# Cached decode attention, two blocks: wq streamed per group, selector matmuls replaced by a DVE transpose, QK matmuls widened

## Chip, cores and metric

The kernel runs on one core of a Trainium2 chip. The metric is the device time of one execution in microseconds (us); runs of one kernel agree within 0.3%, most within 0.1%. Times quoted are medians. "Profile" means the trace of one execution, and the times read from it are from that execution's own start.

The engines in it are PE (TensorE, matrix multiplication; PEld is its loading of the stationary operand), DVE (VectorE), ACT (ScalarE), POOL (GpSimd) and SP (SyncE, which here issues the loads). The loads themselves are moved by 16 DMA engines. QK is the multiplication of the query with the keys, PV that of the probabilities with the values. PSUM is the memory into which PE writes. A slot is on-chip memory for one tile.

## The reference

Two independent blocks, A and B, do the same with their own inputs; the outputs are concatenated.

```python
B, Sq, D = 8, 1, 1024;  H, Sk, Dh = 32, 4096, 128      # all bfloat16
q      = (x @ wq) as [B, H, 1, Dh]
scores = einsum("bhqd,bhkd->bhqk", q, k_cache) * Dh ** -0.5
p      = softmax(scores)
o      = einsum("bhqk,bhkd->bhqd", p, v_cache)
out    = o as [B, 1, H * Dh] @ wo
```

One query per batch means that every key and value is used once: 2 blocks x 32 heads x 8 batches x 2 caches = 1,024 tiles of 1 MB, and besides them 16 MB of wq and 16 MB of wo. The profile counts 1,107 MB read.

## The kernel before

All loads are issued by SP in one fixed order: x and all of wq, then for every head 8 key tiles, a slice of wo, 8 value tiles. A load waits only until its slot is free.

```python
NK = 5                                                   # key slots
NV = 6                                                   # value slots
# ...
wq_sb = sb("wq_sb", [128, NCH, HD], BF16)                # all 8 MB of one block
q_pad = sb("q_pad", [128, NBLK, HD], BF16)
l32 = sb("l32", [128, 2, 8, 4, 32], BF16)
# ... SP:
def prologue_loads(blk):
    # blk 0: wait for the constants, blk 1: for the q of block A
    sp.dma_start(x_sb[0:Bsz, blk, :], x[:, 0, :]).then_inc(s_x[blk], 16)
    for ch in range(NCH):
        sp.dma_start(wq_sb[:, ch, :], wq[ch * 128:(ch + 1) * 128, :]).then_inc(s_wq[blk], 16)
prologue_loads(0)
for n in range(NH):
    for b in range(Bsz):
        wait(sp, s_tr, t - NK + 1)                       # slot free: its tile is transposed
        sp.dma_start(knat[:, slot, :], kc[b, h]...)
    # ... wo
    for b in range(Bsz):
        wait(sp, s_pv, t - NV + 1)                       # slot free: its PV is done
        sp.dma_start(vnat[:, slot, :], vc[b, h]...)
    if blk == 0 and h == H_PRO:                          # head 15: x and wq of block B
        prologue_loads(1)
```

Per key tile, DVE transposes it (2.31 us by the page) and PE multiplies. The stationary operand `l32` has 32 columns, and four matmuls at a time go to four column groups of the array, where they run side by side: the 4,096 columns of a tile took 0.66 us at full clock, and 1.91 us in the changed kernel, whose QK has no column groups:

```python
for c in range(4):
    for g in range(4):
        pe.matmul(S_ps[par][32 * g:32 * g + 32, :], lhsT=l32[:, par, b, c, :],
                  rhs=ktv[:, 8 * g:8 * g + 8, bq, :, e_],          # 256 columns
                  start=(b == 0 and c == 0), stop=(b == Bsz - 1 and c == 3),
                  tile_position=(0, 32 * g))
```

After the eight tiles of a head there is a chain: row maximum (DVE), exchange of the maximum over partitions (PE, DVE, PE), exp (ACT), then the probabilities are brought to the layout that PV needs by 32 selector matmuls and an ACT copy:

```python
for jj in range(8):
    for a_ in range(4):
        pe.matmul(Pn_ps[32 * a_:32 * a_ + 32, jj * 32:(jj + 1) * 32],
                  lhsT=e_sb[:, jj * 32:(jj + 1) * 32], rhs=sel[:, a_, :], ...)
# ACT: pn_sb <- Pn_ps
```

PV is 8 matmuls of 512 columns per value tile, with 4-column stationary operands, batch b in column group b % 4. The output projection adds one head's part to PSUM.

## Time and profile before

| | before |
|---|---|
| time, median of 3 runs | 2685.14 us |
| DMA, steady state | about 419 GB/s, engines 90% busy or more in all slices but the first and the last |
| PE, DVE, ACT busy | 57%, 47%, 10% |
| mean granted PE clock | 0.695 |

From the page of the kernel before: busy time of each engine, then the 40 slices of the span (PEclk is the granted PE clock and DMA the busy share of the 16 DMA engines, in tenths), then two DMA queues with packets, MB and share of 16 engines' span.

```profile
PE 1542.8 (57%) x17024; PEld 603.9 (22%) x17024; DVE 1269.5 (47%) x717; ACT 273.3 (10%) x791; POOL 12.3 (0%) x17
...
PEclk9767767667676776766766767767767667667667
DMA  6999999999999999999999999999999999999998
GB/s 284 409 420 420 418 419 419 418 419 416 420 420 419 419 415 420 417 419 420 416 419 418 419 417 419 416 420 420 419 420 417 420 420 416 418 418 420 413 421 355
...
q1 hardware_dynamic: 159008, 1107.40, 99.7%
q8 instruction: 135, 2.21, 0.3%
```

The DMA row is full except in the first and last slice, and the load queue q1 fills 99.7% of the engines' time. So the kernel waits for bytes, and only two things can shorten it: engines that carry loads in more of the span, or loads that cost the engines less. q8 is the fetch of instructions, 135 packets of 16 KB.

Where the loads are missing is seen in the windows of the start (busy time of PE, weight loads, DVE, ACT, POOL with counts, then granted clock, DMA share, GB/s) ...

```profile
core 0: us, PE busy (x) PEld busy (x) DVE busy (x) ACT busy (x) POOL busy (x), PEclk, DMA share, GB/s
0.00:10.00 10.00, 0.00 (x0) 0.00 (x0) 3.88 (x8) 0.00 (x0) 9.41 (x7) 1.00 0.00 0
10.00:20.00 10.00, 0.38 (x32) 0.33 (x32) 0.90 (x5) 1.51 (x2) 2.90 (x11) 1.00 0.55 209
...
50.00:60.00 10.00, 4.58 (x84) 2.46 (x86) 4.80 (x3) 2.27 (x6) 0.00 (x0) 0.92 0.38 133
```

... and in the timeline of the kernel before (start, duration, engine, line, operation, count):

```profile
2.53 6.93 POOL L193 MEMSET q_pad<- 128x8192 bf16 x1
...
13.01 0.40 SPq L160 DMA_DIRECT2D x_sb<-in_A_x_dram  x1
13.47 4.02 SPq L162 DMA_DIRECT2D wq_sb<-in_A_wq_dram  x8
...
17.53 3.92 SPq L172 DMA_DIRECT2D knat<-in_A_k_cache_dram  x4
```

The first load is issued at 13.0 us, behind POOL's fill of q_pad. At 50 to 60 us the share falls to 0.38: the key slots are full, and PE is still making q for all 32 heads.

Two readings of PE from the middle of the run: a value tile's 8 matmuls, and a key tile's 16 at full and at half clock.

```profile
1003.75 1.89 PE L361 MATMUL ps<-vnat,pn_sb 128*4 128x512 bf16 x8 [0.59 <-DMA vnat<-in_A_v_cache_dram]
...
1011.07 0.66 PE L314 MATMUL ps<-kt,l 128*32 128x256 bf16 x16 [0.90 <-DVE kt L234]
...
1018.52 1.04 PE L314 MATMUL ps<-kt,l 128*32 128x256 bf16 x16 [1.43 <-DVE kt L234]
```

And the time from a load's issue to its landing (the last column, median), which says how much work the DMA engines have queued (a tile lands every 2.483 us, so 12.2 us are about five):

```profile
knat<-in_A_k_cache_dram SPq DMA_DIRECT2D x256, 1024.0 KB, 12.2
vnat<-in_A_v_cache_dram SPq DMA_DIRECT2D x256, 1024.0 KB, 15.3
```

A landing of a 1 MB tile every 2.483 us and 0.68 us for a head's slice of wo make 16 x 2.483 + 0.68 = 40.41 us per head. Every head has one reciprocal on DVE, so the first and the last of the 64 mark the start, the middle and the tail; these are the lines of the timeline before:

```profile
72.90 0.17 DVE L246 RECIPROCAL rlo_sb<-ps 128x2 f32<-128x2 f32 x1 [1.81 <-PE ps L343]
...
2663.07 0.17 DVE L246 RECIPROCAL rlo_sb<-ps 128x2 f32<-128x2 f32 x1 [1.81 <-PE ps L343]
```

The middle is 2663.07 - 72.90 = 2590.2 us. Take from it 63 heads of 40.41 us (2545.8) and the 8 MB of block B's wq (8 x 2.483 = 19.9), and 24.5 us are left. This is the **excess**.

### The profile page before, as it was taken

The page shows a single profiled execution, that of the slowest core. Times are in us where ns is not written, and L with a number is a line of the kernel's source. Part 1 is how long each engine was busy: PE and PEld are TensorE (multiplying, and loading weights), DVE is VectorE, ACT ScalarE, POOL GpSimd, SP SyncE. Part 2 cuts the span into 40 slices and gives each one's busy share as a digit, 9 for nine tenths or more (in the row PEclk, how much of TensorE's full clock was granted, in tenths as well). Part 3 has the DMA queues.
Part 4 walks back from the last instruction along what each step waited for, and adds up shares of the span by engine and source line. Part 5 has one row for each costly group of instructions (what it writes and reads, how often), then busy time and mean ns, then how long its engine had stood idle before and what let it go on. Part 6 is the DMA issues. An engine that isn't in the chain of part 4 may idle for free.

```text
span 2685.2 us, 38364 instructions
## 1 busy us (share of the span) xinstructions
PE 1542.8 (57%) x17024; PEld 603.9 (22%) x17024; DVE 1269.5 (47%) x717; ACT 273.3 (10%) x791; POOL 12.3 (0%) x17
## 2 busy tenths in 40 slices
PE   3655655656465565565665655655655656656555
PEld 1222222222122222222222222222222222222222
DVE  3455354354335435445445445355454454454453
ACT  1100100110011011000110100100100110001001
POOL 1000000000000000000000000000000000000000
PEclk9767767667676776766766767767767667667667
DMA  6999999999999999999999999999999999999998
GB/s 284 409 420 420 418 419 419 418 419 416 420 420 419 419 415 420 417 419 420 416 419 418 419 417 419 416 420 420 419 420 417 420 420 416 418 418 420 413 421 355
DMA packets 159237, 1109.89 MB, mean 413 GB/s; under 512 B 17712, under 2 KB 17744, under 8 KB 25952
## 3 DMA queue, kind: packets, MB, share of 16 engines
q1 hardware_dynamic: 159008, 1107.40, 99.7%
q8 instruction: 135, 2.21, 0.3%
q14 instruction: 30, 0.25, 0.0%
q10 hardware_dynamic: 64, 0.03, 0.0%
HBM read 1107.33 MB, written 0.03 MB: 412 GB/s over the span
## 4 chain that ended last, share of the span: by engine, by line
DMA 60%; PE 18%; DVE 14%; SPq 3%; issue 3%; ACT 1%; POOL 0%; POOLq 0%; DVEq 0%
DMA knat<-in_B_k_cache_dram 30%; DMA knat<-in_A_k_cache_dram 29%; DVE kt L234 11%; PE ps L361 11%; PE ps L314 3%; SPq L172 2%; DVE negm L242 2%; DVE m_sb L238 1%; PE ps L335 1%; SPq L183 1%; DMA wq_sb<-in_A_wq_dram 1%; PE ps L322 1%; PE ps L288 1%; PE ps L273 1%; PE ps L343 1%
## 5 line engine op out<-in xcount | busy, mean ns | idle before, releaser
L234 DVE STREAM_TRANSPOSE kt<-knat 128x2048 f32<-128x2048 f32 x512 | 1183.1, 2311 | 1173.1 <-DMA knat<-in_A_k_cache_dram 589.5
L361 PE MATMUL ps<-vnat,pn_sb 128*4 128x512 bf16 x4096 | 867.3, 436 | 120.7 <-DMA vnat<-in_A_v_cache_dram 60.1
L314 PE MATMUL ps<-kt,l 128*32 128x256 bf16 x8192 | 519.4, 397 | 699.7 <-DVE kt L234 697.8
L314 PEld LDWEIGHTS ps<-kt,l 128*32 128x32 bf16 x8192 | 225.3, 122 | 979.9 <-DVE kt L234 922.1
L361 PEld LDWEIGHTS ps<-vnat,pn_sb 128*4 128x4 bf16 x4096 | 289.0, 92 | 668.9 <-issue 172.9
L450 ACT ACTIVATE o_sb<-ps,rlo_sb 128x512 bf16<-128x512 f32 x128 | 81.0, 684 | 900.3 <-PE ps L361 900.3
L431 ACT ACTIVATE bias_sb<-ps 128x1 f32<-128x1 f32 x64 | 11.0, 171 | 1346.1 <-PE ps L327 1346.1
L419 ACT ACTIVATE l<-ps 32x32 bf16<-32x32 f32 x256 | 76.8, 300 | 33.8 <-PE ps L288 29.1
L372 PE MATMUL ps<-selrow,o_sb 128*128 128x4 bf16 x512 | 22.6, 166 | 87.0 <-ACT o_sb L450 87.0
L246 DVE RECIPROCAL rlo_sb<-ps 128x2 f32<-128x2 f32 x64 | 10.9, 171 | 115.9 <-PE ps L343 115.9
L238 DVE TENSOR_REDUCE m_sb<-ps 128x1 bf16<-128x256 f32 x64 | 27.3, 427 | 73.7 <-PE ps L314 73.7
L335 PE MATMUL ps<-sel,e_sb 128*32 128x32 bf16 x2048 | 26.0, 190 | 56.0 <-ACT e_sb L435 56.0
L242 DVE TENSOR_REDUCE negm<-ps 1x32 bf16<-1x512 f32 x64 | 43.4, 678 | 22.9 <-PE ps L322 22.9
L273 PE MATMUL ps<-wq_sb,xT_sb 128*8 128x512 bf16 x128 | 33.1, 416 | 36.2 <-DMA wq_sb<-in_A_wq_dram 20.7
L372 PEld LDWEIGHTS ps<-selrow,o_sb 128*128 128x128 bf16 x512 | 17.0, 96 | 119.2 <-ACT o_sb L450 119.2
L327 PE MATMUL ps<-scalecol,negm 128*32 128x1 bf16 x256 | 12.5, 186 | 49.3 <-DVE negm L242 49.3
L322 PE MATMUL ps<-ident,m_sb 128*1 128x128 bf16 x64 | 17.0, 266 | 34.2 <-DVE m_sb L238 34.2
L383 PE MATMUL ps<-wo_sb,oT_sb 128*8 128x512 bf16 x128 | 25.2, 390 | 17.1 <-ACT oT_sb L454 17.1
L335 PEld LDWEIGHTS ps<-sel,e_sb 128*32 128x32 bf16 x2048 | 19.1, 104 | 61.4 <-ACT e_sb L435 61.4
L288 PE MATMUL ps<-ident,q_pad 128*32 128x8 bf16 x1024 | 18.3, 172 | 24.2 <-DVE rlo_sb L246 24.2
L435 ACT ACTIVATE e_sb<-ps,bias_sb 128x256 bf16<-128x256 f32 x64 | 30.3, 474 | 2.1
L442 ACT ACTIVATE pn_sb<-ps 128x256 bf16<-128x256 f32 x64 | 24.6, 384 | 14.4 <-PE ps L335 14.4
(39 smaller groups left out, 151.1 us busy)
## 6 DMA issues: line engine op xcount, KB each, us to landing
knat<-in_A_k_cache_dram SPq DMA_DIRECT2D x256, 1024.0 KB, 12.2
vnat<-in_A_v_cache_dram SPq DMA_DIRECT2D x256, 1024.0 KB, 15.3
knat<-in_B_k_cache_dram SPq DMA_DIRECT2D x256, 1024.0 KB, 12.1
vnat<-in_B_v_cache_dram SPq DMA_DIRECT2D x256, 1024.0 KB, 15.5
wq_sb<-in_A_wq_dram SPq DMA_DIRECT2D x8, 1024.0 KB, 11.8
wo_sb<-in_A_wo_dram SPq DMA_DIRECT2D x32, 256.0 KB, 10.4
wq_sb<-in_B_wq_dram SPq DMA_DIRECT2D x8, 1024.0 KB, 16.9
wo_sb<-in_B_wo_dram SPq DMA_DIRECT2D x32, 256.0 KB, 10.4
```

The costliest lines, as they stand in the source:

```text
L172: sp.dma_start(knat[:, slot, :], kc[b, h].rearrange("(p j) d -> p (j d)", p=128),).then_inc(s_kld[slot], 16)
L234: dve.transpose(kt[:, ts, :].bitcast(F32), knat[:, ks, :].bitcast(F32)).then_inc(s_tr, 1)
L238: dve.tensor_reduce(m1_sb[:], S_ps[par], axis=AX.X, op=ALU.max).then_inc(s_m1, 1)
L242: dve.tensor_reduce(negm[0:1, :].rearrange("p (i a) -> p i a", i=8), r_in, axis=AX.XY, op=ALU.max, negate=True).then_inc(s_negm, 1)
L273: last = pe.matmul(q_ps[G % 2], lhsT=xT_sb[:, blk, ch, :], rhs=wq_sb[:, ch, gq * GW:(gq + 1) * GW], start=(ch == 0), stop=(ch == NCH - 1))
L288: last = pe.matmul(qW_ps[32 * a_:32 * a_ + 32, c * 8:c * 8 + 8], lhsT=q_pad[:, blk, base:base + 63:2], rhs=ident[:, 0:8], start=True, stop ...
L314: last = pe.matmul(S_ps[par][32 * g:32 * g + 32, :], lhsT=l32[:, par, b, c, :], rhs=ktv[:, 8 * g:8 * g + 8, bq, :, e_], start=(b == 0 and ...
L322: pe.matmul(R_ps, lhsT=m1_sb[:, 0:1], rhs=ident[:, :], start=True, stop=True).then_inc(s_row, 1)
L335: last = pe.matmul(Pn_ps[32 * a_:32 * a_ + 32, jj * 32:(jj + 1) * 32], lhsT=e_sb[:, jj * 32:(jj + 1) * 32], rhs=sel[:, a_, :], start=True, ...
L361: last = pe.matmul(O_ps[slot][32 * cg:32 * cg + 4, :], lhsT=pn_sb[:, col:col + 4], rhs=vv[:, jj], start=(jj == 0), stop=(jj == 7), tile_po ...
L419: act.activation(dst, src, ACT.Identity).then_inc(s_l32, 1)
L450: act.activation(o_sb[:, slot, :], O_ps[slot], ACT.Identity, scale=rlo_sb[:, slot:slot + 1]).then_inc(s_oev, 1)
```

## The change

The intent: (1) wq is loaded per group of four heads, two heads ahead of its use, so that the first query needs 1 MB and not 8; this frees on-chip memory for more slots (6 and 8). (2) The selector matmuls and the ACT copy become one DVE transpose of the probabilities. For this the scores are laid out 128 x 512, and (3) QK becomes 8 matmuls of 512 columns per tile with a stationary operand of 128 columns, most of them zero, without column groups. Core of the diff, shortened and with my comments:

```diff
-NK = 5
+NK = 6
-NV = 6
+NV = 8
+LEAD = 2
+LW = 132
 ...
-        wq_sb = sb("wq_sb", [128, NCH, HD], BF16)
+        wq_sb = sb("wq_sb", [128, 2, NCH, GW], BF16)
-        q_pad = sb("q_pad", [128, NBLK, HD], BF16)
-        l32 = sb("l32", [128, 2, 8, 4, 32], BF16)
+        q_pad = sb("q_pad", [128, 2, GW], BF16)
+        lpad = sb("lpad", [128, 8, 4, LW], BF16)
 ...
+            def load_group(G):
+                wait(sp, s_qps, G - 1)
                 for ch in range(NCH):
-                    sp.dma_start(wq_sb[:, ch, :], wq[ch * 128:(ch + 1) * 128, :]).then_inc(s_wq[blk], 16)
+                    sp.dma_start(wq_sb[:, G % 2, ch, :],
+                                 wq[ch * 128:(ch + 1) * 128, g * GW:(g + 1) * GW]).then_inc(s_wq[G % 2], 16)
+            load_group(first[0])                  # before the wait for the constants
+            wait(sp, s_const, 1)
 ...
-                        for g in range(4):
+                        for g in range(2):
                             last = pe.matmul(
-                                S_ps[par][32 * g:32 * g + 32, :],
-                                lhsT=l32[:, par, b, c, :],
-                                rhs=ktv[:, 8 * g:8 * g + 8, bq, :, e_],
-                                start=(b == 0 and c == 0), stop=(b == Bsz - 1 and c == 3),
-                                tile_position=(0, 32 * g))
+                                S_ps[par],
+                                lhsT=lpad[:, b, c, 2 - 2 * g:2 - 2 * g + 128],
+                                rhs=ktv[:, 16 * g:16 * g + 16, bq, :, e_],
+                                start=(b == 0 and c == 0 and g == 0),
+                                stop=(b == Bsz - 1 and c == 3 and g == 1))
 ...
-                for jj in range(8):                # 32 selector matmuls, then the ACT copy
-                    for a_ in range(4):
-                        last = pe.matmul(Pn_ps[...], lhsT=e_sb[...], rhs=sel[:, a_, :], ...)
+                dve.transpose(pq_sb[:], e_sb[:]).then_inc(s_pq, 1)
```

More of the change, by code (lines that the diff above doesn't have):

```diff
@@ L40, in bass_concat_heads__mha_block_cached__mha_block_cached__decode_kernel @@
     assert Sq == 1 and S == 4096 and Dh == 128
-    assert 1 <= Bsz <= 8 and D % 128 == 0 and D <= 1024
+    assert 1 <= Bsz <= 8 and D % 128 == 0 and D <= 2048
     NCH = D // 128
@@ L48, in bass_concat_heads__mha_block_cached__mha_block_cached__decode_kernel, with group_of_head, head_of_group @@
     NOC = D // OW
+    assert NOC <= 4
     NBLK = 2
     NH = NBLK * H
+    NGT = NBLK * NG
     SCALE = float(Dh) ** -0.5
-    H_PRO = (H - 1) // 2
+    def group_of_head(n):
+        blk, h = divmod(n, H)
+        return blk * NG + h // HPG
+    def head_of_group(G):
+        blk, g = divmod(G, NG)
+        return blk * H + g * HPG
+    groups_at = {}
+    for G in range(NGT):
+        a = max(head_of_group(G) - LEAD, -1)
+        groups_at.setdefault(a, []).append(G)
     es = ExitStack()
@@ L68, in bass_concat_heads__mha_block_cached__mha_block_cached__decode_kernel @@
         xT_sb = sb("xT_sb", [128, NBLK, NCH, 8], BF16)
-        q_pad = sb("q_pad", [128, NBLK, HD], BF16)
-        l32 = sb("l32", [128, 2, 8, 4, 32], BF16)
+        q_pad = sb("q_pad", [128, 2, GW], BF16)
+        lpad = sb("lpad", [128, 8, 4, LW], BF16)
         ident = sb("ident", [128, 128], BF16)
         ones_bf = sb("ones_bf", [128, 128], BF16)
-        sel = sb("sel", [128, 4, 32], BF16)
         selrow4 = sb("selrow4", [128, 4, 4], BF16)
@@ L85, in bass_concat_heads__mha_block_cached__mha_block_cached__decode_kernel @@
         bias_sb = sb("bias_sb", [128, 1], F32)
-        e_sb = sb("e_sb", [128, 256], BF16)
+        e_sb = sb("e_sb", [128, 512], BF16)
         l1_sb = sb("l1_sb", [128, 1], F32)
@@ L89, in bass_concat_heads__mha_block_cached__mha_block_cached__decode_kernel @@
         rlo_sb = sb("rlo_sb", [128, 2], F32)
-        pn_sb = sb("pn_sb", [128, 256], BF16)
+        pq_sb = sb("pq_sb", [128, 512], BF16)
         o_sb = sb("o_sb", [128, 2, 512], BF16)
         oT_sb = sb("oT_sb", [128, 8], BF16)
-        out_sb = sb("out_sb", [40, NBLK, OW], BF16)
+        out_sb = sb("out_sb", [128, NBLK, OW], BF16)
         ps = es.enter_context(nc.psum_tensor("ps", [128, 8, 512], F32))
-        assert NOC <= 4
-        S_ps = [ps[:, 0, 0:256], ps[:, 0, 256:512]]
-        O_ps = [ps[:, 1, :], ps[:, 2, :]]
-        Pn_ps = ps[:, 3, 0:256]
+        S_ps = [ps[:, 0, :], ps[:, 1, :]]
+        O_ps = [ps[:, 2, :], ps[:, 3, :]]
         R_ps = ps[0:1, 4, 0:128]
@@ L113, in bass_concat_heads__mha_block_cached__mha_block_cached__decode_kernel @@
         s_wold = [sem(f"s_wold{i}") for i in range(NWO)]
-        s_x = [sem(f"s_x{i}") for i in range(NBLK)]
-        s_wq = [sem(f"s_wq{i}") for i in range(NBLK)]
-        s_outdma = [sem(f"s_outdma{i}") for i in range(NBLK)]
+        s_wq = [sem(f"s_wq{i}") for i in range(2)]
+        s_x = sem("s_x")
+        s_outdma = sem("s_outdma")
         s_const = sem("s_const")
@@ L130, in bass_concat_heads__mha_block_cached__mha_block_cached__decode_kernel @@
         s_rlo = sem("s_rlo")
-        s_pnps = sem("s_pnps")
-        s_pn = sem("s_pn")
+        s_pq = sem("s_pq")
         s_pv = sem("s_pv")
@@ L138, in bass_concat_heads__mha_block_cached__mha_block_cached__decode_kernel @@
         s_qwps = sem("s_qwps")
-        s_l32 = sem("s_l32")
+        s_lp = sem("s_lp")
         s_xtps = sem("s_xtps")
@@ L153, in _ @@
         def _(sp):
-            def prologue_loads(blk):
-                x, _, _, wq, _ = blocks[blk]
-                if blk == 0:
-                    wait(sp, s_const, 1)
-                else:
-                    wait(sp, s_qps, NG)
-                sp.dma_start(x_sb[0:Bsz, blk, :], x[:, 0, :]).then_inc(s_x[blk], 16)
-                for ch in range(NCH):
-                    sp.dma_start(wq_sb[:, ch, :], wq[ch * 128:(ch + 1) * 128, :]).then_inc(s_wq[blk], 16)
-            prologue_loads(0)
+            def load_group(G):
+                blk, g = divmod(G, NG)
+                wq = blocks[blk][3]
+                wait(sp, s_qps, G - 1)
+                for ch in range(NCH):
+                    sp.dma_start(wq_sb[:, G % 2, ch, :],
+                                 wq[ch * 128:(ch + 1) * 128, g * GW:(g + 1) * GW]).then_inc(s_wq[G % 2], 16)
+            first = groups_at.get(-1, [])
+            if first:
+                load_group(first[0])
+            wait(sp, s_const, 1)
+            for blk in range(NBLK):
+                sp.dma_start(x_sb[0:Bsz, blk, :], blocks[blk][0][:, 0, :]).then_inc(s_x, 16)
+            for G in first[1:]:
+                load_group(G)
             for n in range(NH):
@@ L175, in _ @@
                     ).then_inc(s_kld[slot], 16)
+                for G in groups_at.get(n, []):
+                    load_group(G)
                 ws = n % NWO
@@ L186, in _ @@
                     ).then_inc(s_vld[slot], 16)
-                if blk == 0 and h == H_PRO:
-                    prologue_loads(1)
         @block.gpsimd
@@ L193, in _ @@
             pool.memset(q_pad[:], 0.0)
-            pool.memset(l32[:], 0.0)
+            pool.memset(lpad[:], 0.0)
             pool.memset(negm[:], 0.0)
@@ L204, in _ @@
             pool.memset(scalecol[0:1, :], SCALE)
+            pool.memset(negm[0:1, :].rearrange("p (i x) -> p i x", x=2)[:, :, 1:2], -30000.0)
             pool.affine_select(ident[:], ones_bf[:], pattern=[[-1, 128]], compare_op=ALU.is_equal,
-                               fill=0.0, base=0, channel_multiplier=1)
-            pool.affine_select(sel[:].rearrange("p a (i g) -> p a i g", i=8), ones_bf[:].rearrange("p (a i g) -> p a i g", a=4, i=8),
-                               pattern=[[-1, 4], [-4, 8], [-32, 4]], compare_op=ALU.is_equal,
                                fill=0.0, base=0, channel_multiplier=1)
@@ L240, in _ @@
                 wait(dve, s_biasps, n)
-                r_in = bass.AP(ps_t, R_ps.offset, [[PS_PSTRIDE, 1], [4, 8], [0, 4], [32, 4], [1, 4]])
-                dve.tensor_reduce(negm[0:1, :].rearrange("p (i a) -> p i a", i=8), r_in, axis=AX.XY, op=ALU.max,
-                                  negate=True).then_inc(s_negm, 1)
+                r_in = bass.AP(ps_t, R_ps.offset, [[PS_PSTRIDE, 1], [4, 8], [0, 2], [32, 4], [2, 2]])
+                dve.tensor_reduce(negm[0:1, :].rearrange("p (i x y) -> p i x y", i=8, x=2)[:, :, :, 0], r_in,
+                                  axis=AX.XY, op=ALU.max, negate=True).then_inc(s_negm, 1)
+                dve.wait_ge(s_exp, n + 1)
+                wait(dve, s_pv, n * Bsz)
+                dve.transpose(pq_sb[:], e_sb[:]).then_inc(s_pq, 1)
                 dve.wait_ge(s_lq, n + 1)
@@ L251, in _, with xT_mm @@
             pe.wait_ge(s_cdve, 3)
-            def prologue_xT(blk):
-                pe.wait_ge(s_x[blk], 16)
+            def xT_mm(blk):
                 wait(pe, s_xt, blk)
@@ L263, in prologue_xT, with qgroup_mm @@
                 last.then_inc(s_xtps, 1)
-            def prologue_qgroup(blk, gq):
-                G = blk * NG + gq
-                if gq == 0:
-                    pe.wait_ge(s_xt, blk + 1)
-                    pe.wait_ge(s_wq[blk], 16 * NCH)
+            def qgroup_mm(G):
+                blk, g = divmod(G, NG)
+                pe.wait_ge(s_xt, blk + 1)
+                pe.wait_ge(s_wq[G % 2], 16 * NCH * (G // 2 + 1))
                 wait(pe, s_q, G - 1)
@@ L273, in prologue_qgroup @@
                     last = pe.matmul(q_ps[G % 2], lhsT=xT_sb[:, blk, ch, :],
-                                     rhs=wq_sb[:, ch, gq * GW:(gq + 1) * GW],
+                                     rhs=wq_sb[:, G % 2, ch, :],
                                      start=(ch == 0), stop=(ch == NCH - 1))
@@ L279, in prep @@
                 blk, h = divmod(n, H)
-                pe.wait_ge(s_q, blk * NG + h // HPG + 1)
-                wait(pe, s_l32, 4 * n)
+                G = group_of_head(n)
+                pe.wait_ge(s_q, G + 1)
+                wait(pe, s_lp, 4 * n)
                 wait(pe, s_rlo, n)
+                hl = h % HPG
                 last = None
@@ L285, in prep @@
                     bq, e_ = c // 2, c % 2
-                    base = h * 128 + 64 * bq + e_
+                    base = hl * 128 + 64 * bq + e_
                     for a_ in range(4):
@@ L289, in prep @@
                             qW_ps[32 * a_:32 * a_ + 32, c * 8:c * 8 + 8],
-                            lhsT=q_pad[:, blk, base:base + 63:2],
+                            lhsT=q_pad[:, G % 2, base:base + 63:2],
                             rhs=ident[:, 0:8], start=True, stop=True, tile_position=(0, 32 * a_))
                 last.then_inc(s_qwps, 1)
-            prologue_xT(0)
-            for gq in range(NG):
-                prologue_qgroup(0, gq)
+            pe.wait_ge(s_x, 16 * NBLK)
+            for blk in range(NBLK):
+                xT_mm(blk)
+            for G in groups_at.get(-1, []):
+                qgroup_mm(G)
             prep(0)
@@ L306, in _ @@
                     if b == 0:
-                        pe.wait_ge(s_l32, 4 * (n + 1))
-                        wait(pe, s_exp, n)
+                        pe.wait_ge(s_lp, 4 * (n + 1))
+                        wait(pe, s_exp, n - 1)
                     ktv = kt[:, ts, :].rearrange("p (j q pp e) -> p j q pp e", j=32, q=2, pp=32, e=2)
@@ L329, in _ @@
                 last.then_inc(s_biasps, 1)
-                pe.wait_ge(s_exp, n + 1)
-                wait(pe, s_pn, n)
-                last = None
-                for jj in range(8):
-                    for a_ in range(4):
-                        last = pe.matmul(Pn_ps[32 * a_:32 * a_ + 32, jj * 32:(jj + 1) * 32],
-                                         lhsT=e_sb[:, jj * 32:(jj + 1) * 32], rhs=sel[:, a_, :],
-                                         start=True, stop=True, tile_position=(0, 32 * a_))
-                last.then_inc(s_pnps, 1)
                 pe.wait_ge(s_l1m, n + 1)
@@ L345, in _ @@
                 last.then_inc(s_lq, 1)
-                prep_late = (blk == 0 and h == H - 1 and H_PRO == H - 1)
-                if n + 1 < NH and not prep_late:
+                if n + 1 < NH:
                     prep(n + 1)
@@ L353, in _ @@
                     if b == 0:
-                        pe.wait_ge(s_pn, n + 1)
+                        pe.wait_ge(s_pq, n + 1)
                         wait(pe, s_oev, 2 * n)
                     cg, slot = b % 4, b // 4
-                    vv = vnat[:, vs, :].rearrange("p (g jj d) -> p jj g d", g=4, jj=8)
                     last = None
-                    for jj in range(8):
-                        col = jj * 32 + 4 * b
+                    for u in range(8):
+                        g, jq = u // 4, u % 4
+                        base = 32 * 4 * jq + 4 * b + 2 * g
+                        j0 = 16 * g + 4 * jq
                         last = pe.matmul(O_ps[slot][32 * cg:32 * cg + 4, :],
-                                         lhsT=pn_sb[:, col:col + 4], rhs=vv[:, jj],
-                                         start=(jj == 0), stop=(jj == 7), tile_position=(0, 32 * cg))
+                                         lhsT=pq_sb[:, base:base + 97:32], rhs=vnat[:, vs, j0 * 128:(j0 + 4) * 128],
+                                         start=(u == 0), stop=(u == 7), tile_position=(0, 32 * cg))
                     last.then_inc(s_pv, 1)
@@ L366, in _ @@
                 wait(pe, s_ot, n)
-                if n + 1 < NH and not prep_late:
-                    pe.wait_ge(s_l32, 4 * (n + 2))
+                if n + 1 < NH:
+                    pe.wait_ge(s_lp, 4 * (n + 2))
                 last = None
@@ L385, in _ @@
                 last.then_inc(s_op, 1)
-                if blk == 0:
-                    if h == H_PRO:
-                        prologue_xT(1)
-                    for gq in range(NG):
-                        if h == min(H_PRO + gq, H - 1):
-                            prologue_qgroup(1, gq)
-                if n + 1 < NH and prep_late:
-                    prep(n + 1)
+                for G in groups_at.get(n, []):
+                    qgroup_mm(G)
         @block.scalar
@@ L398, in _, with xT_copy, qgroup_copy, lpad_copies @@
             act.wait_ge(s_cdve, 3)
-            def prologue_xT(blk):
+            def xT_copy(blk):
                 act.wait_ge(s_xtps, blk + 1)
                 act.activation(xT_sb[:, blk, :, :].rearrange("p c b -> p (c b)"), xT_ps, ACT.Identity).then_inc(s_xt, 1)
-            def prologue_qgroup(blk, gq):
-                G = blk * NG + gq
+            def qgroup_copy(G):
                 act.wait_ge(s_qps, G + 1)
-                act.activation(q_pad[0:8, blk, gq * GW:(gq + 1) * GW], q_ps[G % 2], ACT.Identity).then_inc(s_q, 1)
-            def l32_copies(n):
-                par = n % 2
+                if G >= 2:
+                    act.wait_ge(s_qwps, head_of_group(G - 2) + HPG)
+                act.activation(q_pad[0:8, G % 2, :], q_ps[G % 2], ACT.Identity).then_inc(s_q, 1)
+            def lpad_copies(n):
                 act.wait_ge(s_qwps, n + 1)
-                wait(act, s_qk, (n - 1) * Bsz)
-                l32t = l32[:].tensor
-                pstride = l32[:].ap[0][0]
+                wait(act, s_qk, n * Bsz)
+                lpt = lpad[:].tensor
+                pstride = lpad[:].ap[0][0]
                 for a_ in range(4):
-                    off = l32[32 * a_:32 * a_ + 32, par, 0, 0, a_:a_ + 1].offset
-                    dst = bass.AP(l32t, off, [[pstride, 32], [4 * 32 + 4, 8], [32, 4]])
+                    off = lpad[32 * a_:32 * a_ + 32, 0, 0, 32 * a_ + 2:32 * a_ + 3].offset
+                    dst = bass.AP(lpt, off, [[pstride, 32], [4 * LW + 4, 8], [LW, 4]])
                     src = qW_ps[32 * a_:32 * a_ + 32, :].rearrange("p (c b) -> p b c", c=4)
-                    act.activation(dst, src, ACT.Identity).then_inc(s_l32, 1)
-            prologue_xT(0)
-            for gq in range(NG):
-                prologue_qgroup(0, gq)
-            l32_copies(0)
+                    act.activation(dst, src, ACT.Identity).then_inc(s_lp, 1)
+            for blk in range(NBLK):
+                xT_copy(blk)
+            for G in groups_at.get(-1, []):
+                qgroup_copy(G)
+            lpad_copies(0)
             for n in range(NH):
@@ L432, in _ @@
                 act.wait_ge(s_actb, n + 1)
-                wait(act, s_pnps, n)
+                wait(act, s_pq, n)
                 wait(act, s_l1m, n)
@@ L439, in _ @@
                 act.activation(l1m_sb[:], maskslot[:], ACT.Identity, scale=l1_sb[:]).then_inc(s_l1m, 1)
-                act.wait_ge(s_pnps, n + 1)
-                wait(act, s_pv, n * Bsz)
-                act.activation(pn_sb[:], Pn_ps, ACT.Identity).then_inc(s_pn, 1)
-                prep_late = (blk == 0 and h == H - 1 and H_PRO == H - 1)
-                if n + 1 < NH and not prep_late:
-                    l32_copies(n + 1)
+                if n + 1 < NH:
+                    lpad_copies(n + 1)
                 act.wait_ge(s_pv, (n + 1) * Bsz)
@@ L461, in _ @@
                         act.dma_start(out[:, 0, blk * D + c * OW:blk * D + (c + 1) * OW],
-                                      out_sb[32 * c:32 * c + Bsz, blk, :]).then_inc(s_outdma[blk], 16)
-                if blk == 0:
-                    if h == H_PRO:
-                        prologue_xT(1)
-                    for gq in range(NG):
-                        if h == min(H_PRO + gq, H - 1):
-                            prologue_qgroup(1, gq)
-                if n + 1 < NH and prep_late:
-                    l32_copies(n + 1)
-            for blk in range(NBLK):
-                act.wait_ge(s_outdma[blk], 16 * NOC)
+                                      out_sb[32 * c:32 * c + Bsz, blk, :]).then_inc(s_outdma, 16)
+                for G in groups_at.get(n, []):
+                    qgroup_copy(G)
+            act.wait_ge(s_outdma, 16 * NOC * NBLK)
 _INS = ['A_x', 'A_k_cache', 'A_v_cache', 'A_wq', 'A_wo', 'B_x', 'B_k_cache', 'B_v_cache', 'B_wq', 'B_wo']
```

## The prediction

> **What bounds it now.** The DMA engines. The page's slices show them 90% busy or more from the second on, at about 419 GB/s; the DMA table puts the load queue at 99.7% of 16 engines' span; 59% of the chain of waits is key loads. PE is busy 57%, DVE 47%. In the timeline a 1 MB tile lands every 2.48 us; 16 of them and 256 KB of wo (0.68 us) make 40.4 us per head. So 1,024 tiles, 64 wo slices and 16 MB of wq need about 2,626 us of transfers that the change does not shrink. The other 59 us, from windows and landing times:
> - start: the first load is issued at 13.0 us, after POOL's fills (q_pad alone 6.9 us);
> - 7 us of missing transfers at 50 to 80 us (DMA share 0.38 in 50:60): all key slots are full while PE makes q for 32 heads;
> - about 27 us over the heads: mean period 40.8, not 40.4. The engines' landings of one tile drift apart when an instruction-fetch packet passes (135 of 16 KB, 1.07 us each);
> - tail: about 7.6 us after the last landing.
>
> **What the change does.**
> 1. wq per group: 1 MB, not 8, before the first query, issued before POOL is done. q_pad's fill shrinks eightfold, l's doubles: constants ready at about 8.5 us, not 13. Worth 4 to 7 us, plus the 7 us stall.
> 2. Cost: wq comes in 1 KB rows and 128 DMAs. In the trace a packet of 8 KB took 312 ns, of 2 KB 84, of 1 KB (the output) 46: about 7 ns more than its share of an 8 KB packet. 16,384 rows over 16 engines: 7 us, plus 1 us of completions. [...]
> 3. QK loses its column tiling: 8 matmuls of 512 columns per tile instead of 16 of 256 that ran four abreast. From 0.66 us (full clock) or 1.05 (half) to about 1.9, as PV's 8 matmuls take now: 500 us more PE time. It stays under 2.48, so it costs nothing while the clock is full. It should be: [...] PV at 1.89 of every 2.48 us holds clock 1.00 while sparse QK falls to 0.50. Estimated head without DMA: QK 17, chain 4, PV 14 to 16, rest 2.5: 38 to 39.5, under 40.4.
> 4. Selector matmuls (0.41) and the ACT copy (0.38) go, a DVE transpose (about 0.6) comes, reduce and exp widen, the row reduce narrows. The chain of 3.8 us stays near 4, hidden.
> 5. About 36% fewer PE instructions (34,000 to 21,800): about 85 fetch packets. With slots 6/8, not 5/6, engines may drift further without starving. I expect 27 us to become about 12.
>
> **Sum.** 2685 - 6 - 7 - 15 + 8 = about 2,665 us. Range 2,650 to 2,682. Faster by over 2%: 0.02; within 2%: 0.95; slower: 0.03.
>
> **Right if:** no DMA dip at 50:60; first key load near 9 us; QK near 1.9 us per tile; PE busy near 2,000 us, clock well above 0.70; fetch packets near 85; head period near 40.5, more in heads with a wq group.
>
> **Wrong if:** the clock falls in the K phase (8 x 0.43 = 3.4 us per tile, over 2.48), so that PE bounds; weight loads of 128 columns do not hide; 1 KB rows read slower than packets show; the drift does not come from instruction fetch.

The sum: 2685 - 6 (start) - 7 (stall) - 15 (excess) + 8 (wq), about 2,665 us. The 8 us are worked out from the trace of the kernel before: 16,384 rows over 16 engines at 7 ns more each, and 112 more loads, each with 16 packets of 4 bytes of 9 ns, one for an engine. That the clock would stay full under the wide QK was my estimate, from the clock of 1.00 beside PV and 0.50 beside the old QK. The head without DMA was an estimate too, from 1.9 us a tile for QK, 1.89 for PV and 3.8 us for the chain.

## The result

| | before | after |
|---|---|---|
| time, median (runs) | 2685.34 us (12) | 2669.56 us (10) |
| ratio | | 0.9941, 95% interval 0.9931 to 0.9950 |
| PE busy, clock | 1542.8 us, 0.695 | 2007.7 us, 0.931 |
| instruction-fetch packets | 135 | 87 |

A ratio is the mean time of one kernel's fast runs over that of the other's in the same rounds, so it is not quite the ratio of the medians. Its interval lies below 1, so the kernel is faster, and by less than 2%. The forecast of 2,665 us, with a range of 2,650 to 2,682, held; the saving was 15.8 us by the medians and not 20.

The lines of the page of the changed kernel that answer to those above (q1's share adds up the packets' times, and the sum can pass 100%):

```profile
PE 2007.7 (75%) x10880; PEld 728.6 (27%) x10880; DVE 1292.2 (48%) x781; ACT 263.6 (10%) x727; POOL 7.7 (0%) x17
...
PEclk9998999999989899999899998999999999999999
DMA  9999999999999999999999999999999999999998
GB/s 370 417 421 421 417 421 417 421 420 416 420 415 421 421 417 421 415 421 420 414 421 417 420 420 415 420 416 420 419 419 421 415 420 413 420 420 418 420 420 350
...
q1 hardware_dynamic: 175136, 1107.41, 100.5%
q8 instruction: 87, 1.43, 0.2%
```

The windows and the timeline of its start:

```profile
core 0: us, PE busy (x) PEld busy (x) DVE busy (x) ACT busy (x) POOL busy (x), PEclk, DMA share, GB/s
0.00:10.00 10.00, 0.00 (x0) 0.00 (x0) 4.71 (x13) 0.00 (x0) 7.70 (x17) 1.00 0.37 108
10.00:20.00 10.00, 5.55 (x91) 2.06 (x92) 4.62 (x2) 3.54 (x8) 0.00 (x0) 1.00 0.99 395
...
50.00:60.00 10.00, 6.59 (x33) 2.28 (x33) 4.09 (x2) 1.44 (x3) 0.00 (x0) 0.94 1.01 418
```

```profile
0.82 3.70 SPq L171 DMA_DIRECT2D wq_sb<-in_A_wq_dram  x8
...
2.55 0.95 POOL L210 MEMSET q_pad<- 128x1024 bf16 x1
3.44 3.62 POOL L211 MEMSET lpad<- 128x4224 bf16 x1
...
8.40 0.35 SPq L179 DMA_DIRECT2D x_sb<-in_A_x_dram  x1
...
9.11 10.01 SPq L189 DMA_DIRECT2D knat<-in_A_k_cache_dram  x8
```

The dip at 50 to 60 us is gone, wq's first megabyte is issued at 0.8 us, and the first key at 9.1 us, once POOL's constants are done.

The same two readings of PE, a value tile and then key tiles (the first two of a head in one stretch, begun at half clock, then one at full clock):

```profile
1047.41 1.89 PE L372 MATMUL ps<-vnat,pq_sb 128*4 128x512 bf16 x8 [0.59 <-DMA vnat<-in_A_v_cache_dram]
...
1052.25 5.23 PE L334 MATMUL ps<-kt,lpad 128*128 128x512 bf16 x16 [0.58 <-DVE kt L249]
...
1060.40 1.91 PE L334 MATMUL ps<-kt,lpad 128*128 128x512 bf16 x8 [0.28 <-DVE kt L249]
```

A key tile now takes 1.91 us in the median, just as forecast from PV, which is under 2.48 us. It does not always stay there: the granted clock was 0.52 at 1052 to 1054 us, when the head's keys began, and in 41 of the 512 tiles, each the first or second of its head, QK took more than 2.48 us (up to 3.57). The other six of every head took 1.9 us, so PE catches up within the head.

Issue to landing, and the first and last reciprocal:

```profile
knat<-in_A_k_cache_dram SPq DMA_DIRECT2D x256, 1024.0 KB, 26.5
vnat<-in_A_v_cache_dram SPq DMA_DIRECT2D x256, 1024.0 KB, 20.9
```

```profile
41.82 0.17 DVE L264 RECIPROCAL rlo_sb<-ps 128x2 f32<-128x2 f32 x1
...
2647.08 0.17 DVE L264 RECIPROCAL rlo_sb<-ps 128x2 f32<-128x2 f32 x1
```

The two profiles give the account below. 15 of the 16 wq groups fall into the middle. Each is counted as 8 loads of 0.375 us, 3.0 us, the estimate behind the forecast. The landings in the trace bear it out: from the last load before a group to the fourth after it, less 2.484 us for every tile and 0.68 us for wo, a group adds 2.96 us (median of the 15).

| term | before | after | difference |
|---|---|---|---|
| to the first reciprocal, without block A's wq (19.9) | 53.0 | 41.8 | -11.2 |
| wq in A's start and in the middle | 39.7 | 45.0 | +5.3 |
| 63 heads at 40.41 | 2545.8 | 2545.8 | 0 |
| excess of the middle | 24.5 | 14.4 | -10.1 |
| after the last reciprocal | 22.1 | 20.4 | -1.7 |
| span | 2685.2 | 2667.5 | -17.7 |

The spans of the profiles differ by 17.7 us and the medians of the runs by 15.8. The profiled execution before took 2686.9 us, 1.6 over the median of its runs; the one after took 2669.3 us, 0.3 under its. So 2 us of the table are chance between runs, and in which term they lie is not known.

### The profile page after: what moved, and what is told of

It is laid out like the page before. It is cut to its first block, busy times and chain, and to the rows that moved or that the text cites. A ratio compares the mean times of both kernels' runs of the same rounds, so it can differ in the third digit from the quotient of the medians.

```text
span 2667.5 us, 26152 instructions
## 1 busy us (share of the span) xinstructions
PE 2007.7 (75%) x10880; PEld 728.6 (27%) x10880; DVE 1292.2 (48%) x781; ACT 263.6 (10%) x727; POOL 7.7 (0%) x17
## 4 chain that ended last, share of the span: by engine, by line
DMA 81%; DVE 9%; SPq 7%; PE 2%; issue 1%; ACT 0%; POOL 0%; DVEq 0%; POOLq 0%; ACTq 0%
DMA knat<-in_B_k_cache_dram 40%; DMA knat<-in_A_k_cache_dram 36%; DVE kt L249 9%; SPq L189 3%; DMA vnat<-in_A_v_cache_dram 3%; DMA vnat<-in_B_v_cache_dram 2%; SPq L171 2%; SPq L202 2%; PE ps L334 1%; PE ps L289 1%; SPq L197 0%; PE ps L372 0%; POOL lpad L211 0%; ACT o_sb L452 0%; PE ps L394 0%
## 5 line engine op out<-in xcount | busy, mean ns | idle before, releaser
L334 PE MATMUL ps<-kt,lpad 128*128 128x512 bf16 x4096 | 1023.5, 394 | 226.3 <-DVE kt L249 224.3
L372 PE MATMUL ps<-vnat,pq_sb 128*4 128x512 bf16 x4096 | 845.1, 429 | 124.4 <-DMA vnat<-in_B_v_cache_dram 63.3
L334 PEld LDWEIGHTS ps<-kt,lpad 128*128 128x128 bf16 x4096 | 367.9, 99 | 873.9 <-DVE kt L249 445.8
L372 PEld LDWEIGHTS ps<-vnat,pq_sb 128*4 128x4 bf16 x4096 | 290.9, 94 | 648.6 <-issue 140.5
L253 DVE TENSOR_REDUCE m_sb<-ps 128x1 bf16<-128x512 f32 x64 | 44.4, 694 | 128.6 <-PE ps L334 128.6
L261 DVE STREAM_TRANSPOSE pq_sb<-e_sb 128x512 bf16<-128x512 bf16 x64 | 45.5, 711 | 83.7 <-ACT e_sb L441 83.7
L424 ACT ACTIVATE lpad<-ps 32x32 bf16<-32x32 f32 x256 | 78.0, 305 | 70.2 <-PE ps L306 65.5
L354 PE MATMUL ps<-l1m_sb,maskcg 128*32 128x2 f32 x512 | 16.5, 188 | 90.5 <-ACT l1m_sb L445 90.5
L441 ACT ACTIVATE e_sb<-ps,bias_sb 128x512 bf16<-128x512 f32 x64 | 44.0, 687 | 2.1
L289 PE MATMUL ps<-wq_sb,xT_sb 128*8 128x512 bf16 x128 | 39.5, 465 | 0.0
L257 DVE TENSOR_REDUCE negm<-ps 1x16 bf16<-1x128 f32 x64 | 18.0, 281 | 19.7 <-PE ps L342 19.7
## 6 DMA issues: line engine op xcount, KB each, us to landing
knat<-in_A_k_cache_dram SPq DMA_DIRECT2D x256, 1024.0 KB, 26.5
vnat<-in_A_v_cache_dram SPq DMA_DIRECT2D x256, 1024.0 KB, 20.9
wq_sb<-in_A_wq_dram SPq DMA_DIRECT2D x64, 128.0 KB, 10.1
```

The source lines that it names most:

```text
L253: dve.tensor_reduce(m1_sb[:], S_ps[par], axis=AX.X, op=ALU.max).then_inc(s_m1, 1)
L261: dve.transpose(pq_sb[:], e_sb[:]).then_inc(s_pq, 1)
L289: last = pe.matmul(q_ps[G % 2], lhsT=xT_sb[:, blk, ch, :], rhs=wq_sb[:, G % 2, ch, :], start=(ch == 0), stop=(ch == NCH - 1))
L334: last = pe.matmul(S_ps[par], lhsT=lpad[:, b, c, 2 - 2 * g:2 - 2 * g + 128], rhs=ktv[:, 16 * g:16 * g + 16, bq, :, e_], start=(b == 0 and ...
L372: last = pe.matmul(O_ps[slot][32 * cg:32 * cg + 4, :], lhsT=pq_sb[:, base:base + 97:32], rhs=vnat[:, vs, j0 * 128:(j0 + 4) * 128], start=( ...
L424: act.activation(dst, src, ACT.Identity).then_inc(s_lp, 1)
```

## The experiments

Twelve runs were made, ten with four or five timed executions each, in rounds with the kernel before, and the last two with one look each.

### 1. Taking the change apart

The forecast gave the shrinking excess to two causes at once: fewer instruction fetches and deeper slots. The first theory is *fetch*: each fetch packet delays one DMA engine, and the loads go at the pace of the latest. Its rival is *slots*: only the depth of the queues matters.

**after_again** is the changed kernel once more, without an edit. 

> The changed kernel once more, as the partner of the three runs beside it. About 2,669 us; 87 instruction-fetch packets; mean head period without the wq loads 0.2 us over 40.4.

Measured: 2669.8 us, excess 15.6 us. It is "the changed kernel beside it" of the next three runs. The excess of one kernel thus differs by 1.2 us between two of its profiles.

**stream_only** has the new loads and slots but the old compute (the edit in words, as for the next run):

```diff
 NK = 6; NV = 8; wq per group                      # as in the changed kernel
-   QK with lpad, 8 x 512 columns; dve.transpose(pq_sb, e_sb)
+   QK with l32, 16 x 256 columns in 4 column groups; 32 selector matmuls; ACT copy
```

> wq per group and slots 6/8 as in the changed kernel, but the old compute (column-tiled QK, selector matmuls), so about 135 fetch packets. Fetch theory: the start gains all of its 14 us, wq costs 8, but the drift stays near 25 us, so about 2,679 us. Slot theory (deeper buffers shrank the drift): about 2,669 us, as the changed kernel. If the wide QK itself cost time, this run would be faster than the changed kernel.

Measured: 2676.6 us, 135 fetch packets, excess 24.8 us. It is 6.8 us slower than the changed kernel beside it, at 441 us less PE busy time (1566.7 against 2007.7).

**compute_only** has the new compute, but wq whole and slots 5/6. To make room in the on-chip memory, two small tensors that are used only for constants were laid into `e_sb`:

```diff
 NK = 5; NV = 6; wq whole                          # as before
-   QK with l32, 16 x 256 columns in 4 column groups; 32 selector matmuls; ACT copy
+   QK with lpad, 8 x 512 columns; dve.transpose(pq_sb, e_sb)
```

> The new compute (wide QK, DVE transpose) with wq loaded whole as before and slots 5/6, so about 87 fetch packets. Fetch theory: start and stall as before, drift down from 25 to about 15 us: about 2,675 us. Slot theory: the drift stays, about 2,685 us.

Measured: 2693.4 us, 7.7 us *slower* than before (ratio 1.0029, interval 1.0016 to 1.0042). Its five executions lie further apart than those of the other kernels, from 2689.0 to 2696.0 us. Both theories missed. 2.9 us of it lie before the first reciprocal (75.8 against 72.9 us); part of that is that the wider zero fill of lpad comes before the first load, as the timeline of this run shows (before: 13.01 us):

```profile
9.41 3.62 POOL L192 MEMSET lpad<- 128x4224 bf16 x1
...
14.37 0.39 SPq L158 DMA_DIRECT2D x_sb<-in_A_x_dram  x1
```

The excess was 29.1 us, although the fetch packets were 86. So fewer packets alone did not help at this depth.

**slots56** is the changed kernel with the old slots:

```diff
-NK = 6
-NV = 8
+NK = 5
+NV = 6
```

> The changed kernel with 5 key and 6 value slots instead of 6 and 8. Fetch theory: within 2 us of the changed kernel, about 2,670 us. Slot theory: the drift comes back to about 25 us, about 2,679 us.

Measured: 2676.0 us, 6.2 us slower than the changed kernel beside it, excess 21.2 us. Its issue-to-landing times show the shorter queue (changed kernel: 26.5 and 20.9):

```profile
knat<-in_A_k_cache_dram SPq DMA_DIRECT2D x256, 1024.0 KB, 11.6
vnat<-in_A_v_cache_dram SPq DMA_DIRECT2D x256, 1024.0 KB, 14.2
```

So neither theory stood alone: the gain in the excess needs both the fewer instructions and the deeper slots, and putting either back costs 6 to 7 us. The reading that fits all four: the new compute gains nothing by itself; it pays by way of its smaller instruction count, once the slots are there, and the slots stand where wq did (its tensor shrank from 8 MB to 2). (Wide QK and DVE transpose were not run apart from each other.) That compute_only has a larger excess than slots56 (29.1 against 21.2), with the same compute and slots, is not explained by any run; compute_only's executions spread by 7 us and those of slots56 by 4, so part of it may be chance.

### 2. Where the excess comes from

The completion counts show it more closely. In the trace every load raises its semaphore sixteen times; taken as one rise for each of the 16 DMA engines, the sixteen times of one load give the engines' places. Going through all 1 MB tiles between 100 and 2,640 us and adding up every landing that came more than 0.12 us later than 2.484 us after the one before gives (worked out from the trace, not a view of the profile):

```
run            late landings   sum us   of them within 7 us after a fetch packet of q8 (share of time so covered)
before               45         25.5        43 landings, 25.1 us   (0.36)
stream_only          35         22.8        35 landings, 22.8 us   (0.37)
slots56              43         21.1        35 landings, 19.5 us   (0.24)
compute_only         52         31.1        39 landings, 27.4 us   (0.23)
after                13         15.1        13 landings, 15.1 us   (0.23)
```

In the changed kernel all of the excess follows a fetch. That is a coincidence in time far beyond chance, but not yet a cause. So fetches were added.

**pool_fills192** and **pool_fills480** let the idle POOL execute one-element fills, which nothing reads, in every head:

```diff
+            for n in range(NH):
+                pool.wait_ge(s_row, n + 1)
+                wait(pool, s_pf, n)
+                for i in range(192):                 # or 480
+                    fill = pool.memset(scratch[:, i:i + 1], 0.0)
+                fill.then_inc(s_pf, 1)
```

> The changed kernel with 192 one-element fills per head on the idle POOL: as many more instructions as PE lost by the change, about 135 fetch packets in all instead of 87, and nothing else. Fetch theory (each fetch packet delays one DMA engine, and the loads go at the pace of the latest): the excess over 40.4 us a head goes from 15 to about 24 us, as in the run with the old compute and the same slots, so about 2,678 us. If fetches are only a marker: 2,669 us.

> 480 fills per head, about 207 fetch packets. Fetch theory: at 0.17 us a packet the excess is about 36 us, so about 2,690 us. Marker: 2,669 us.

Measured: 2725.6 and 2827.0 us, ratios to the kernel before of 1.015 and 1.053. The direction is that of the fetch theory, the size is not: 56 and 157 us more than the changed kernel instead of 9 and 21. The DMA queue tables of the two runs, and then of the changed kernel, tell why:

```profile
q8 instruction: 86, 1.41, 0.2%
q14 instruction: 128, 1.04, 0.1%
```

```profile
q8 instruction: 87, 1.43, 0.2%
q14 instruction: 271, 2.22, 0.2%
```

```profile
q8 instruction: 87, 1.43, 0.2%
q14 instruction: 30, 0.25, 0.0%
```

POOL's instructions come on queue q14 (98 and 241 packets more than the 30 of the changed kernel), in packets of 8 KB and not on q8 in packets of 16 KB as PE's. The excess is 68.8 and 169.3 us; over the 14.4 us of the changed kernel this is 0.56 and 0.64 us for each added packet. The completion counts of five loads in the run with 192 fills show what one of them does:

```
load landed at us   first of 16 engines to last   first to last but one
1011.47                     5.65                         1.74
1013.95                     5.65                         1.74
1017.07                     6.28                         1.74
1052.54                     6.29                         1.73
1055.65                     6.91                         1.74
```

Fifteen engines keep their places; one, and always the same one, falls back by 0.63 us at each packet, and every load waits for it. With PE's packets it goes otherwise: in the kernel before, 13 packets between 240 and 490 us delayed an engine by 1.4 to 1.7 us each, and by following the engines from load to load these delays fell on about eight different ones in turn. (The trace has no engine numbers; that the places belong to the same engine from load to load is inferred from their staying constant.) An estimate from this: 135 packets on eight engines at 1.5 us are 25 us for each, and 87 packets 16 us. Measured were 24.5 and 24.8 us with 135 packets, and 14.4 and 15.6 with 87 packets and deep slots.

The fills also write to the on-chip memory, and no run has the one without the other. The trace of pool_fills192 tells them apart in time: between 100 and 2,640 us the last engine's lag behind the first grew by 0.45 to 0.9 us from one load to the next 84 times. All 84 loads landed within 3.3 us after the start of a q14 packet, and in 35 of the 84 cases no fill ran in the 2.5 us before the landing. So the steps follow the packets and not the writes. The number of packets fits too: by the pages of the kernels before and after, 12,288 PE instructions fewer (matmuls and weight loads) went with 48 packets of 16 KB fewer, 256 to a packet. From this I estimate 128 to a packet of half that size, and so 1.5 packets for 192 fills and 3.75 for 480; the 98 and 241 added packets are 1.53 and 3.77 for each head.

Whether a fetch costs PE itself any time no run shows. Here, where the loads are the limit, it is paid in their time: (24.8 - 14.4) / 48 = 0.22 us for each of PE's packets between stream_only and the changed kernel, if the whole difference is theirs, and about 0.6 us for each of POOL's.

**slots810** asks whether still deeper slots help:

```diff
-NK = 6
-NV = 8
+NK = 8
+NV = 10
```

> The changed kernel with 8 key and 10 value slots. Slot theory (a late engine is made up for as long as the others still have queued work): the excess falls from 15 us towards 6 us, the 87 packets of 1.07 us spread evenly over 16 engines; I expect about 10 us, 2,664 us. If depth no longer matters: 2,669 us.

Measured: 2669.7 us, as the changed kernel; excess 14.5 us. My even spread over 16 engines did not hold. If about eight engines take the packets in turn, depth cannot bring the excess below what the most delayed engine gets, and 6/8 is deep enough for that; this fits, and no further run tests it.

### 3. The cost of wq in short rows

**wq_2k** loads wq for two groups at once:

```diff
-        wq_sb = sb("wq_sb", [128, 2, NCH, GW], BF16)
+        wq_sb = sb("wq_sb", [128, 2, NCH, 2 * GW], BF16)
 ...
-                                 wq[ch * 128:(ch + 1) * 128, g * GW:(g + 1) * GW]).then_inc(s_wq[G % 2], 16)
+                                 wq[ch * 128:(ch + 1) * 128, g * GW:(g + 2) * GW]).then_inc(s_wq[P % 2], 16)
```

> wq loaded for two groups at once: rows of 2 KB, 64 loads of 256 KB instead of 128 of 128 KB. A 256 KB load in 2 KB rows took 0.67 us and 128 KB in 1 KB rows 0.375, so 14 MB cost 37.5 instead of 42 us, and the first megabyte more lies before the first key load, where the engines were idle. Row-size theory: about 2,664 us. If the rows do not matter: 2,669 us.

Measured: 2663.1 us, ratio 0.9918, 6.5 us less than the changed kernel (both against the same kernel before, in different rounds). The middle is 5.0 us shorter (2600.2 against 2605.3) and the start 1.2; the start is no more than chance, for after_again reached its first reciprocal at 40.8 us and the changed kernel at 41.8. The edit does two things: it lengthens the rows, and it moves one more megabyte out of the middle, in front of the keys. The landings tell them apart. Measured as for the table above, the 2 MB of two groups add 5.40 us here (median of 7), 2.70 for a megabyte against 2.96 in the changed kernel. That is 3.6 us for the 14 MB left in the middle, and the megabyte that was moved is another 3.0. So the row-size theory holds, but rows are only about half of the saving.

### 4. The start

**early_k** issues x and the first keys when x_sb has been zeroed, not when all constants are done:

```diff
-            pool.memset(x_sb[:], 0.0)
+            pool.memset(x_sb[:], 0.0).then_inc(s_xz, 1)
 ...
-            wait(sp, s_const, 1)
+            wait(sp, s_xz, 1)
```

> The changed kernel, but x and the first keys are issued as soon as x_sb is filled with zeros (about 2.6 us) instead of after all constants (8.4 us). Start theory (every microsecond in which the engines have no load at the start is a microsecond of the total): first key load at about 5.3 instead of 9.1 us, so about 3.8 us less, 2,666 us. If the start is hidden behind PE's backlog: 2,669.6 us.

Measured: 2666.1 us, ratio 0.9931; 3.5 us less than the changed kernel, or 2.8 us if each is set against the kernel before in its own rounds (18.6 and 15.8 us under it). The timeline of SP:

```profile
0.81 3.71 SPq L172 DMA_DIRECT2D wq_sb<-in_A_wq_dram  x8
...
5.31 10.85 SPq L190 DMA_DIRECT2D knat<-in_A_k_cache_dram  x8
```

The first key is issued 3.8 us earlier and the time falls by nearly as much.

**early_wq2k** has both edits. 

> Both improvements together: 2 KB rows for wq, and x and keys issued early. If the two add up: 2,663 minus 3 to 4, about 2,659.5 us, 1% under the kernel before. If the second megabyte of wq already fills the gap before the keys, the early issue adds little: 2,662 us.

Measured: 2662.2 us, ratio 0.9916. This is the lowest time found, 22 us under the kernel before, but only 0.9 us under wq_2k, and their executions overlap (2660.8 to 2663.0 us, and 2662.7 to 2663.4): the second of the two forecasts. Two megabytes of wq already use most of the gap in front of the keys: the DMA share at 0 to 10 us was 0.67 in wq_2k and 0.71 in early_wq2k, against 0.37 in the changed kernel.

### 5. How much room the compute has

The forecast put a head without its loads at 38 to 39.5 us, so close under 40.4 that the wide QK looked risky. Two kernels load only a quarter of each tile. Their outputs are wrong, which doesn't matter for the times.

```diff
-                        knat[:, slot, :], kc[b, h].rearrange("(p j) d -> p (j d)", p=128)
+                        knat[:, slot, 0:1024], kc[b, h].rearrange("(p j) d -> p (j d)", p=128)[:, 0:1024]
         # the same for vnat; both filled with zeros once at the start
```

**quarter_wide** has the compute of the changed kernel. 

> Wrong result on purpose: only a quarter of each key and value tile is loaded, so a tile costs the DMA engines 0.67 instead of 2.48 us and the compute of the changed kernel shows its own pace. Predicted 38 to 39.5 us a head (against 40.4 that the loads take). If the wide QK had no room left it would be 40.4 or more.

**quarter_tiled** has the old compute with the new loads. 

> Wrong result on purpose: the same with the old compute (column-tiled QK, selector matmuls) and the changed kernel's loads. The DVE transposes, 2.2 us a tile back to back, pace QK in both, so I expect only 1 to 2 us a head less than with the wide QK: about 36.5 to 38 us.

Measured: the mean distance of two reciprocals is 33.4 us a head with the wide QK and 31.5 with the tiled one (one run of each, 2,210 and 2,088 us). The difference of 1.9 us was as expected, the level was not. Six DVE transposes back to back took 13.29 us in quarter_wide, 2.2 a tile. Groups of quarter_wide (line, engine, operation, tiles, count; busy time, mean of one; idle time before):

```profile
L336 PE MATMUL ps<-kt,lpad 128*128 128x512 bf16 x4096 | 970.5, 380 | 138.6 <-DVE kt L251 137.1 <-ACT lpad L426 1.5
L374 PE MATMUL ps<-vnat,pq_sb 128*4 128x512 bf16 x4096 | 614.6, 434 | 0.4 <-issue 0.2
```

And one head's PV in its timeline:

```profile
1027.45 7.99 PE L374 MATMUL ps<-vnat,pq_sb 128*4 128x512 bf16 x64
```

64 matmuls of 512 columns in 7.99 us are 125 ns each, where I had counted 14 us and more for a head. I read this as neighbouring batches running abreast in their column groups when the value tiles are all there; a tile alone takes 1.89 / 8 = 0.24 us for each. In the real kernel PE waits for each value tile alone, which is why the timelines before and after show 1.89 us a tile. So the wide QK left 7 us of room a head, not 1 to 2.

### All runs

| run | time, us | ratio to before | fetch packets q8 | slots | excess, us |
|---|---|---|---|---|---|
| before | 2685.3 | | 135 | 5/6 | 24.5 |
| after | 2669.6 | 0.9941 | 87 | 6/8 | 14.4 |
| after_again | 2669.8 | 0.9941 | 87 | 6/8 | 15.6 |
| stream_only | 2676.6 | 0.9967 | 135 | 6/8 | 24.8 |
| compute_only | 2693.4 | 1.0029 | 86 | 5/6 | 29.1 |
| slots56 | 2676.0 | 0.9966 | 86 | 5/6 | 21.2 |
| slots810 | 2669.7 | 0.9942 | 86 | 8/10 | 14.5 |
| pool_fills192 | 2725.6 | 1.0150 | 86 and 98 of POOL | 6/8 | 68.8 |
| pool_fills480 | 2827.0 | 1.0531 | 87 and 241 of POOL | 6/8 | 169.3 |
| wq_2k | 2663.1 | 0.9918 | 86 | 6/8 | 16.9 |
| early_k | 2666.1 | 0.9931 | 87 | 6/8 | 13.5 |
| early_wq2k | 2662.2 | 0.9916 | 86 | 6/8 | 14.4 |

(In wq_2k and early_wq2k the 14 MB of wq in the middle are counted as 2.68 us each, four loads of 0.67. The two runs of section 5 stand there.)

## Why the prediction was right

- *What bounds the kernel*: right. DMA stayed full in both, and PE's 465 us more busy time cost nothing that a run shows: quarter_wide is at 33.4 us a head, under 40.4.
- *Step 1, the start*: right. Forecast 13 us for start and stall, with the first megabyte of wq counted in. Measured -11.2 for the start alone; the hidden first megabyte appears in my account as 3 us less in the wq term. early_k supports the reading that time without loads at the start is lost nearly one for one.
- *Step 2, short rows*: right. Forecast +8 for 16 MB. Start and wq together came to -11.2 + 5.3 = -5.9 us, against a forecast of -13 + 8 = -5. From the landings, a megabyte took 2.96 us in 1 KB rows against 2.483 in 8 KB rows, which makes 7.6 us for 16 MB, and 2.70 in the 2 KB rows of wq_2k: row length is the cause.
- *Step 3, wide QK*: right in what it forecast for the tile (1.9 us; 1.91 measured in the median), the clock (0.93, "well above 0.70") and PE (2,007.7 us, "near 2,000"). That the clock would rise was my estimate from the clock beside PV, and the runs bear it out: with QK at 1.91 of 2.48 us the mean granted clock rose from 0.695 to 0.931, and it was 0.69 to 0.71 in every run with the old QK and 0.92 to 0.94 in every run with the wide one. What in the new compute raises it was not shown. The first key tiles of a head still met a low clock (41 tiles over 2.48 us), the case named under "Wrong if", without PE becoming the limit. The estimate of a head without DMA was mis-sized: 33.4 and not 38 to 39.5, because PV was counted at its waiting pace.
- *Step 4, the chain*: right and without weight. From the end of the last QK to the first PV it was 3.8 us before and 3.9 us after. The DVE transpose of the probabilities took 0.71 us, against an estimate of about 0.6.
- *Step 5, the excess*: the term of the sum that was mis-sized. Forecast 27 to 12, a gain of 15; measured 24.5 to 14.4, a gain of 10. The fetch packets were as forecast (87), and that they cause the excess is supported by the POOL runs and by the late landings. Two things were mis-sized: a packet delays its engine by about 1.5 us and not by the 1.07 that its record shows, and PE's packets go to about eight engines in turn, as inferred from the landings in section 2, so that by the estimate there the floor is near 15 us and not 12. That both parts of the change are needed for this gain was not seen at all; I had named them side by side.
- *Not in the forecast*: 1.7 us less in the tail.

The forecast of 20 us was 4.2 too hopeful by the medians. Step 5 is 5 us of that, start and wq and the tail give 2.6 back, and the 1.9 us by which the profiled spans differ more than the medians make up the rest. That the range held says little by itself: stream_only (2676.6) and slots56 (2676.0), each with a part of the change taken out, lie in it too. What supports the forecast is that its steps were measured one by one.

Left open: why compute_only has 8 us more excess than slots56; by what rule fetches are given to DMA engines; and whether PE instructions alone, added to the changed kernel, would bring its excess back. That last run was not made; the added instructions were POOL's, which came on another queue.

## What to carry to other kernels

Here the DMA engines were full, and an edit was worth what it changed in their time: idle start (about 3 us in early_k), row length (2.70 instead of 2.96 us a megabyte in wq_2k), and what else they carry. Instructions were such a load too. With the deeper slots, PE's shorter instruction stream went with 10 us less excess (48 packets fewer), and filling an idle engine with many small instructions cost about 0.6 us for every 128 of them (one packet of 8 KB). Elsewhere it has to be measured again. A part of a change that loses alone (the new compute, slower by 0.3%) can win once another part (freed memory, deeper slots) is there, so test parts both alone and within the whole.
